# Attention with a token MLP: PSUM score banks as a group of three and a group of two plus one bank for VectorE, in place of two groups of three

## The chip, the cores and the metric

The kernel runs on one core of a Trainium2 chip. The metric is the time of one execution on the device in microseconds (us), the median of the runs. Five engines of the core work side by side, each through its own instruction queue: TensorE (PE, matrix products; PEld is its weight loads), VectorE (DVE), ScalarE (ACT), GpSimd (POOL) and SyncE (SP), which issues the transfers (DMA). Matrix products land in PSUM, which this kernel uses as eight banks of 128 rows by 512 fp32 numbers. All other data on the core lie in SBUF.

## The reference

The input x has 2048 rows (tokens) of 640 numbers in bf16. One layer norm feeds an attention block and an MLP that mixes tokens; the MLP's result gates the attention's:

```
xn  = layernorm(x)                                  # no scale, no shift
q,k,v = split(xn @ wqkv)                            # 32 heads of 20 numbers
s   = concat(softmax(q k^T / sqrt(20)) v) @ wo
h   = layernorm(xn)                                 # h^T: 640 x 2048
y   = (gelu(h^T @ w1 + b1) @ w2 + b2)^T             # 2048 -> 1536 -> 2048 over tokens
out = x + s * silu(y)
```

The largest part is the exponential of the scores: 32 heads x 2048 x 2048 numbers.

## The kernel before

**The unit of work.** The heads are taken in 8 sets of four (`NG`, `GH`), the queries in 4 parts of 512 (`NTB`): 32 passes. In a pass the keys are 16 chunks of 128. One unit is one head, one chunk, one part of the queries: a score tile of 128 keys by 512 queries, which fills one PSUM bank. There are 32 x 16 x 4 = 2048 units. A product of depth 32 (L1206, in `emit_st`) makes the tile; the four heads of a set lie in the four row groups of TensorE, so that tiles of different heads can be computed at once and tiles of the same head follow each other. Below, a "score phase" is one call of `emit_st`: the tiles that are issued together.

**Two ways to the exponential.** ScalarE takes the tiles of a whole bank group with one ACTIVATE (L1235, in `emit_exp`), which reads two or three adjacent banks and writes bf16 to `pt_sb`. VectorE takes single tiles and makes the exponential from bit patterns: one TENSOR_SCALAR from PSUM to 16-bit integers (L1246, `emit_op1`; one per unit), and after the four heads of a chunk three TENSOR_SCALARs over all four tiles at once (L1268, `emit_top`), which give three shifted copies. A chunk handled in this way is here called a VectorE chunk; it costs TensorE 16 value products in place of 4. Only the chunks in `RC` (five of a pass's 16) can be VectorE chunks. The value products (L1284, `emit_pv`) collect a pass in one bank.

**Banks.** Bank 6 (`AB`) collects the value products. Bank 7 (`JB`) serves all other products (MLP, projections, output), called jobs, one at a time. Banks 0 to 5 hold score tiles in two groups of three, `ACT_GROUPS`. A group is refilled (`do_st`, L1836) when ScalarE has read it. At the refill the planner may lend the group's last bank to VectorE: then two tiles go to ScalarE and the third to VectorE (`lent`). It lends if VectorE's reckoned backlog (`dve_load`, L1830) is below `LEND` and a VectorE chunk has a head left that the other two tiles don't use. A group with a lent bank can be refilled only when VectorE has read its tile (the test in `pe_cands`, L1665). Besides, VectorE may get a tile in bank 7 when no job holds it (`d_bank`, L1161), with the refill of a group or in a score phase of its own.

**Ramp and tail.** In the first part of the kernel (`ramp`) the layer norm, the transposes and the first projections run. Once the first score tile can be made, the group banks are withdrawn from the jobs. `dveready` is set when the keys of the first set are complete, and `ramp` ends when the last of the first value projections and the last of the first query projections are issued. While `ramp` holds there are neither lent banks nor tiles in bank 7, so VectorE gets no tile. At the end, banks 0 to 5 go to the last output products (`tbank`).

**Who sets the order.** The program is written out ahead of time by a planner (`schedule`). It keeps a clock for each engine with a reckoned cost for each instruction and picks the next instruction by priorities and readiness. On the chip the queues run in that fixed order with semaphores between them. Every 16 score tiles (`WIN`) the planner reads the next row of a table (`PLAN`, 129 rows, applied by `tune`, with the choices of `OPTS`), which sets its 14 options anew: among them `LEND` (the fifth digit of a row), `DRIDE` (how long TensorE may wait so that a tile for VectorE can ride with a refill), `CONFL` (whether a tile that rides may share its head with another of the phase), `PARTS` (value products taken in parts) and `DON` (whether new VectorE chunks may start). The weight loads of the MLP are reckoned at 1.8 times their bytes (`dma_w1`, `dma_w2`: 922 per row of 512 bytes).

Of the kernel before, what the change touches and what calls it, by code (L numbers as in the profile page):

```python
# [260 lines left out]
class _Kern:  # L261
# [4 lines left out]
    NG = 8  # L266
    EPS = 1e-5
    RP = 20
    ACT_GROUPS = ((0, 1, 2), (3, 4, 5))
    AB = 6  # L270
    JB = 7
    RC = (2, 5, 8, 11, 14)
# [12 lines left out]
    CONFL = True  # L285
    FILL, FGAP, FACT = True, 40.0, 0.6
    LATE = 2.0
    LEND, LEND_MIN = 1800.0, 3
    SHARE = True
    VPRIO = 24.0  # L290
    QAT = (0.0, 0.0, 0.0, 0.0)
# [10 lines left out]
        ("MINJ", (640.0, 320.0, 1000.0)),  # L302
        ("ROOM", (3, 6, 0)),
        ("DRIDE", (400.0, 150.0, 700.0)),
        ("LEND", (1800.0, 1300.0, 2400.0, 700.0, 0.0)),
        ("PARTS", ((2,), (2, 1), (3, 1), (1,), ())),
        ("LATE", (2.0, -9.0, 99.0)),
        ("DON", (True, False)),
# [5 lines left out]
        ("GROT", (1, 0)),  # L314
    )
    PLAN = (
        "00000000000010", "00000000000000", "00100000001000", "00000000000000", "10200300000100", "10200300100100",
        "20020000000010", "20022010000010", "10000000000100", "00000100000000", "01000100000100", "00000000000000",
        "20102000000000", "00000000000000", "00000000010000", "01000300010000", "01002310100110", "01010300110000",
        "01010320100000", "01021310100000", "01001310000100", "10000200010000", "10022210011000", "11022220011000",  # L320
        "00103300000010", "00102300000010", "21102000000000", "00000200000010", "20200000000000", "10201000000000",
        "10000200010000", "12000000010000", "00000000000000", "01000000000100", "01022300000100", "00022300010100",
        "02000010000010", "00000000000000", "00200010100010", "00000010110010", "01003000000100", "01000200010100",
        "01000200010100", "10000000100000", "10000010100100", "10100010000100", "01010020011100", "00000000000000",
        "01000200000000", "00000000000000", "00010000110000", "01010010110000", "21010310111000", "22110310111010",
        "00003100001000", "01000000000100", "01000000101100", "01010000101100", "00000000000000", "10000000010100",
        "01000000001110", "00000000001100", "00000000000000", "00001000000000", "22020000000000", "00000000000000",
        "01000000100000", "02000010100000", "01000010100000", "00000000000000", "01000300000000", "11020300000100",
        "11020300000000", "11120100000000", "11120100000010", "11120100010110", "11210100011110", "12210100011110",
        "02210100011010", "11210100001010", "11221100011010", "11201100111010", "11201210111110", "10020420000000",  # L330
        "00000000000000", "02000001010000", "30000000011000", "00000420000000", "00000400000100", "00100000100000",
        "01000200000000", "01000200000000", "00000000000000", "00023000101000", "01000000001000", "00100000000100",
        "00000000000000", "00000020000000", "00000000000000", "00001010000010", "01100000000000", "10000000000000",
        "00000000000000", "00000020100000", "10002320100000", "10200010001000", "10202010001000", "01200110011100",
        "00002000100000", "02002000010000", "00022020010000", "00000000000000", "00001001010100", "00001000111100",
        "00010420000000", "02001000001100", "00000000000000", "20000000100000", "00000300000000", "00104310000000",
        "00000100100010", "10020100100010", "30000100100010", "00002000001000", "01012000000000", "00000000000000",
        "00000320000000", "00022310000000", "00022311000000",
    )
    PARTS = (2,)  # L340
    DX = (1, 2, 3)
# [74 lines left out]
    def schedule(self):  # L416
# [14 lines left out]
        PROW = 4096  # L431
        A_x, A_wqkv, A_wo, B_w1, B_b1, B_w2, B_b2, out = (self.A_x, self.A_wqkv, self.A_wo, self.B_w1,
                                                          self.B_b1, self.B_w2, self.B_b2, self.out)
        AB, JB = self.AB, self.JB
        RC, NR = self.RC, len(self.RC)
        sl = {}

# [11 lines left out]
        done = set()  # L449
# [516 lines left out]

        jobs = []
        bankq = []
        freebanks = [3, 4, 5, 0, 1, 2, JB]
        retired = set()  # L970
        busybanks = set()
        active = []
# [85 lines left out]
        dquads = []  # L1058
        tfree = list(range(self.NTILE))
        dlive = [0]  # L1060
        dop1 = []
        lent = set()
        dtop = []
# [58 lines left out]
        def a_left(q):  # L1122
            n = sum(4 for c in range(NB) if (q, c) not in claimed)
            if a_cur[1] is not None and a_cur[0] == q:
                n += GH - a_cur[2]
            return n
# [34 lines left out]
        def d_bank():  # L1161
            if not dveready[0]:
                return None
            if JB in bank_off:
                return None
            if self.SHARE and JB in freebanks and len(dop1) < 2 and not ramp[0]:
                return JB
            return None

        def d_take(g, bk):  # L1170
            d = d_cur[0]
            if d is None:
                q, c, r = d_claimable()
                claimed.add((q, c))
                dlive[0] += 1
                d = d_cur[0] = dict(q=q, c=c, r=r, todo=[0, 1, 2, 3], tl=[tfree.pop(0), None, None, None], fin=[0.0] * 4, left=4, pk=0)
                stats["dve_units"] += 4
                nd_pass[q] += 1
            d["todo"].remove(g)
            if bk == JB:  # L1180
                freebanks.remove(bk)
                busybanks.add(bk)
            else:
                lent.add(bk)
            dop1.append((d, g, bk))
            u = (d["q"], d["c"], g)
            if not d["todo"]:
                d_cur[0] = None
            return u
# [52 lines left out]
        def emit_op1():  # L1242
            d, g, bk = dop1.pop(0)
            w = dt_sb[:, d["tl"][0], g, :]
            src = ps(bk)
            tk = pr.dve(lambda e: e.tensor_scalar(w, src, WOFF, 0.0, ALU.add, ALU.max), reads=[bank_slot[bk]],  # L1246
                   writes=[S_(f"dt{d['tl'][0]}_{g}")], name=f"dw{d['q']}_{d['c']}_{g}", cost=601.0)
            if bk != JB:
                lent.discard(bk)
            else:  # L1250
                busybanks.discard(bk)
                freebanks.append(bk)
                freebanks.sort(reverse=True)
            d["left"] -= 1
            if d["left"] == 0:
                dtop.append([d, 1])
                d["fin"][0] = tk.fin
                if self.EARLY:
                    dquads.append((0.0, d))
# [394 lines left out]
        def fin_bank(b):  # L1654
            return b not in busybanks
# [273 lines left out]
        while True:  # L1929
            guard += 1  # L1930
            if nclaim[0] >= win * self.WIN:
                self.tune(win)
                win += 1
            assert guard < 400000
            if ramp[0] and "v0_14" in done and "qk0_0_3" in done:
                ramp[0] = False
            if not dveready[0] and "qk0_1_3" in done:
                dveready[0] = True
            nomore = next_chunk(a_cur[0], claimed) is None and a_cur[1] is None
            if nomore:  # L1940
                for b in act_banks:
                    if b not in bank_off and b not in lent and not any(b in x[1] for x in pexp):
                        bank_off.add(b)
                        if len(tbank) < 4:
                            done.add(f"tbank{len(tbank)}")
                            tbank.append(b)
            if (nomore or (a_cur[0] == NP - 1 and a_left(NP - 1) < self.D_GUARD)) and d_cur[0] is None and not dop1:
                if not bankq and JB not in busybanks and JB not in bank_off:
                    bank_off.add(JB)
                    done.add(f"bankoff{JB}")  # L1950
            activate()
            order = sorted(("pe", "act", "dve", "pool"), key=lambda e: pr.T[e])
            cs_by = {}
            for e in order:
                cs_by[e] = pe_cands(pr.T[e]) if e == "pe" else eng_cands(e, pr.T[e])
            bt = None
            for e in order:
                if not cs_by[e]:
                    continue
                r = min(max(x[1], pr.T[e]) for x in cs_by[e])  # L1960
                if bt is None or r < bt[0]:
                    bt = (r, e)
            if bt is None:
                break
            r, e = bt
            ok = [x for x in cs_by[e] if x[1] <= r + 1e-6]
            ok.sort(key=lambda x: (x[0], x[1]))
            if pr.T[e] < r:
                pr.T[e] = r
            ok[0][2]()  # L1970
# [41 lines left out]
```

## Time and profile before

| | before |
|---|---|
| median of three runs | 756.44 us (755.57 to 756.48) |
| the profiled execution | 755.57 us, span 753.7 us |
| ScalarE busy | 729.9 us (97%) |
| VectorE busy | 721.0 us (96%) |
| TensorE busy | 717.6 us (95%) |
| exponentials of three banks on ScalarE | 208 |
| exponentials of two banks on ScalarE | 464 |
| score tiles of VectorE | 496 (124 chunks) |
| DMA, mean | 56 GB/s |

The span runs from the first to the last instruction; the time of the execution is 1.9 us longer. "Busy" counts overlapping instructions once. "Idle before" is time in which an engine had nothing to do ahead of an instruction, with what ended it. Matmuls of different row or column groups overlap, so that a busy TensorE is not one at its peak.

### The profile page before, as it was taken

The numbers are of one execution on the slowest core, as the hardware profiler recorded it, in microseconds if no ns is written. First come the engines' busy times: TensorE is split into PE (matmuls) and PEld (weight loads), VectorE is DVE, ScalarE is ACT, GpSimd is POOL, SyncE is SP. The second block draws the span as 40 slices with busy tenths as digits, with TensorE's granted clock in tenths as the row PEclk, the third lists the DMA queues.
The fourth block names the chain that finished last, engine by engine and source line by source line (L and its number), as shares of the span: only waits on it lengthen the run. The fifth ranks groups of instructions, "written<-read, shape, count | busy, mean of one in ns | idle before, by whom it ended". The sixth has DMA issues, their size and how long they took to land.

```text
span 753.7 us, 23158 instructions
## 1 busy us (share of the span) xinstructions
PE 717.6 (95%) x10302; PEld 240.7 (32%) x10302; DVE 721.0 (96%) x1320; ACT 729.9 (97%) x695; POOL 15.6 (2%) x22
## 2 busy tenths in 40 slices
PE   9999999999999999999999999999999988998997
PEld 7432223222323232323223323233333232222222
DVE  8869999999999999999999999999999999999997
ACT  4999999999999999999999999999999999999993
POOL 4200000000000000000000000000000000000001
PEclk9999999999999999999999999999999999999999
DMA  9584111110313031121014022223124340011011
GB/s 245 109 167 57 38 26 38 20 36 7 86 14 77 13 68 38 35 61 21 7 37 111 26 49 52 47 54 102 44 57 82 76 150 11 6 47 48 13 47 36
DMA packets 117143, 42.54 MB, mean 56 GB/s; under 512 B 75300, under 2 KB 115876, under 8 KB 116996
## 3 DMA queue, kind: packets, MB, share of 16 engines
q1 hardware_dynamic: 117044, 41.07, 23.9%
q8 instruction: 80, 1.31, 0.7%
q14 instruction: 19, 0.16, 0.1%
HBM read 26.37 MB, written 10.22 MB: 49 GB/s over the span
## 4 chain that ended last, share of the span: by engine, by line
ACT 85%; PE 12%; DVE 2%; DMA 1%; issue 0%; POOL 0%
ACT pt_sb L1235 83%; PE ps_all L1284 4%; PE ps_all L644 4%; PE ps_all L1206 4%; ACT zt_sb L840 1%; ACT zt_sb L835 1%; PE ps_all L929 1%; DMA xnT_sb<-regC 1%; DVE bst_sb L531 0%; DVE bst_sb L533 0%; DMA regA<-in_A_x_dram 0%; DVE regC L549 0%; DVE regC L1607 0%; PE ps_all L683 0%; DVE xnT_sb L611 0%
## 5 line engine op out<-in xcount | busy, mean ns | idle before, releaser
L1235 ACT ACTIVATE pt_sb<-ps_all 128x1024 bf16<-128x1024 f32 (+1 forms) x672 | 710.5, 1226 | 2.4 <-PE ps_all L1206 1.9
L1246 DVE TENSOR_SCALAR dt_sb<-ps_all 128x512 uint16<-128x512 f32 x496 | 328.2, 684 | 10.1 <-PE ps_all L1206 8.3
L1206 PE MATMUL ps_all<-qk_sb 32*128 32x512 bf16 x2048 | 266.7, 384 | 27.7 <-ACT pt_sb L1235 24.8
L1268 DVE TENSOR_SCALAR dt_sb<-dt_sb 128x2048 uint16<-128x2048 uint16 x372 | 241.9, 687 | 1.4
L1206 PEld LDWEIGHTS ps_all<-qk_sb 32*128 32x128 bf16 x2048 | 67.0, 91 | 283.8 <-ACT pt_sb L1235 231.8
L1284 PE MATMUL ps_all<-dt_sb,vs_sb 128*21 128x512 bf16 x1488 | 124.6, 382 | 0.8 <-DVE dt_sb L1268 0.7
L1284 PE MATMUL ps_all<-pt_sb,v_sb 128*21 128x512 bf16 x1552 | 124.2, 382 | 0.9 <-DVE tr_sb L1400 0.6
L644 PE MATMUL ps_all<-regB,regA 128*32 128x128 bf16 (+1 forms) x1536 | 68.2, 301 | 0.7 <-DVE regB L845 0.3
L644 PE MATMUL ps_all<-regC,regA 128*32 128x512 bf16 (+1 forms) x1536 | 68.4, 301 | 0.0
L1284 PE MATMUL ps_all<-dt_sb,v_sb 128*21 128x512 bf16 x496 | 49.0, 384 | 0.3 <-DVE tr_sb L1400 0.2
L644 PE MATMUL ps_all<-xnT_sb,wqk_sb 128*32 128x512 bf16 x640 | 48.2, 382 | 0.3 <-DVE zt_sb L814 0.2
L1284 PEld LDWEIGHTS ps_all<-dt_sb,vs_sb 128*21 128x21 bf16 x1488 | 31.5, 91 | 41.3 <-issue 21.9
L1284 PEld LDWEIGHTS ps_all<-pt_sb,v_sb 128*21 128x21 bf16 x1552 | 28.7, 90 | 47.7 <-issue 38.0
L644 PEld LDWEIGHTS ps_all<-regB,regA 128*32 128x32 bf16 x1536 | 27.2, 96 | 27.0 <-issue 13.1
L644 PEld LDWEIGHTS ps_all<-regC,regA 128*32 128x32 bf16 x1536 | 27.3, 96 | 25.6 <-issue 13.4
L929 PE MATMUL ps_all<-wv_sb,xnT_sb 128*128 128x128 bf16 (+3 forms) x160 | 29.5, 302 | 0.1
L644 PE MATMUL ps_all<-wv_sb,xnT_sb 128*32 128x480 bf16 x320 | 23.0, 369 | 0.0
L1400 DVE STREAM_TRANSPOSE tr_sb<-ps_all 128x512 f32<-128x512 f32 x31 | 22.1, 711 | 0.9 <-PE ps_all L1284 0.7
L644 PEld LDWEIGHTS ps_all<-xnT_sb,wqk_sb 128*32 128x32 bf16 x640 | 13.7, 95 | 18.2 <-issue 7.7
L1284 PEld LDWEIGHTS ps_all<-dt_sb,v_sb 128*21 128x21 bf16 x496 | 12.6, 90 | 21.3 <-issue 14.7
L814 DVE TENSOR_SCALAR zt_sb<-ps_all,b2h_sb 128x512 bf16<-128x512 f32 (+1 forms) x32 | 17.2, 544 | 0.0
L1044 DVE CAST v_sb<-ps_all 128x480 bf16<-128x480 f32 (+1 forms) x22 | 13.4, 610 | 3.3 <-PE ps_all L737 3.1
(82 smaller groups left out, 307.0 us busy)
## 6 DMA issues: line engine op xcount, KB each, us to landing
regA<-in_B_w_dram SPq DMA_DIRECT2D x6, 1024.0 KB
regA<-in_B_w_dram SPq DMA_DIRECT2D x8, 768.0 KB
qk_sb<-qk_scratch_dram SPq DMA_DIRECT2D x56, 80.0 KB
qk_scratch_dram<-qs_sb SPq DMA_DIRECT2D x32, 128.0 KB
regA<-in_A_x_dram SPq DMA_DIRECT2D x6, 640.0 KB
ok_scratch_dram<-on_sb SPq DMA_DIRECT2D x96, 20.0 KB
out_dram<-regC SPq DMA_DIRECT2D x3, 640.0 KB
wqk_sb<-in_A_wqkv_dram SPq DMA_DIRECT2D x2, 480.0 KB
```

The source lines that it names most:

```text
L644: fns.append(lambda e, c=c, e_=e_: e.matmul(oc(c, e_), lhsT[:, c:e_], rhs, start=start, stop=stop, tile_position=(0, c)))
L814: steps.append(("dve", lambda e, z=z, i=i, jj=jj: e.tensor_scalar(z[:, c0:c0 + n], ps(bk, n, i * n), 0.5, bias[:, jj:jj + 1], ALU.mult, AL ...
L835: steps.append(("act", lambda e: e.activation(tt_, tt_, AF.Tanh, scale=1.5957691216), [stt], [stt], f"th{j}", ac(n)))
L840: steps.append(("act", lambda e: e.activation(tt_, z, AF.Tanh), sz, [stt], f"th2_{j}", ac(n)))
L929: steps.append(("pe", lambda e, c=c, k=k: e.matmul(ap, oT_sb[0:k, c, b * 128:(b + 1) * 128], wo_ap[0:k, c, c0:c0 + n], start=(opens and c ...
L1044: return lambda e: e.tensor_copy(dst, src)
L1206: pr.pe(lambda e, outp=outp, lhsT=lhsT, rhs=rhs, g=g: e.matmul(outp, lhsT, rhs, start=True, stop=True, tile_position=(32 * g, 0)), reads=[ ...
L1235: tk = pr.act(lambda e: e.activation(outp, inp, AF.Exp, scale=math.log(2.0) / 128.0), reads=[bank_slot[b] for b in banks[:n]], writes=[S_( ...
L1246: tk = pr.dve(lambda e: e.tensor_scalar(w, src, WOFF, 0.0, ALU.add, ALU.max), reads=[bank_slot[bk]], writes=[S_(f"dt{d['tl'][0]}_{g}")], n ...
L1268: tk = pr.dve(lambda e: e.tensor_scalar(dst, src, dk, None, ALU.add), reads=[S_(f"dt{b0}_{g}") for g in range(4)], writes=[S_(f"dt{b}_{g}" ...
L1284: pr.pe(lambda e: e.matmul(outp, lhsT, rhs, start=(k == 0), stop=last, tile_position=(0, 32 * g)), reads=reads, writes=[bank_slot[AB]], na ...
L1400: steps.append(("dve", lambda e: e.transpose(tr_sb[:, :], ps(AB)), [bank_slot[AB]], [S_("tr")], f"epT{q}", 632.0))
```

## The change

Banks 0 to 5 are divided anew: ScalarE has a group of three (0, 1, 2) and a group of two (3, 4), and bank 5 becomes `DB`, a bank for VectorE's tiles alone. `d_bank` offers it first, whenever it is empty, without asking whether the ramp has ended. Until `dveready` is set, bank 5 serves jobs; after that it is withdrawn from them. The group of three may still lend its third bank (`LEND_MIN` is 3), the group of two never. At the end bank 5 joins the banks of the last output products.

The table is another one throughout: all 129 rows differ, and the choices for `LEND` are now 900, 300, 1500, 0 and 2500 ns in place of 1800, 1300, 2400, 700 and 0. Of the 129 rows before, 95 chose 1800, 18 chose 2400, 11 chose 1300, 4 chose 700 and 1 chose 0. After, 82 choose 900, 17 choose 1500, 16 choose 0 (never lend), 8 choose 2500 and 6 choose 300. Three rows before forbid new VectorE chunks (`DON`), none after. The reckoned weight loads are the same in both versions.

```diff
-    ACT_GROUPS = ((0, 1, 2), (3, 4, 5))
+    ACT_GROUPS = ((0, 1, 2), (3, 4))
+    DB = 5
...
-    LEND, LEND_MIN = 1800.0, 3
+    LEND, LEND_MIN = 1100.0, 3
...
-        ("LEND", (1800.0, 1300.0, 2400.0, 700.0, 0.0)),
+        ("LEND", (900.0, 300.0, 1500.0, 0.0, 2500.0)),
...
     PLAN = (
-        "00000000000010", "00000000000000", "00100000001000", "00000000000000", "10200300000100", "10200300100100",
+        "00010000000000", "00000000000000", "00000000000010", "00000000000000", "01020420000000", "01210300000000",
...
-        freebanks = [3, 4, 5, 0, 1, 2, JB]
+        freebanks = [3, 4, DB, 0, 1, 2, JB]
...
+        dbank = ["free"]
...
         def d_bank():
             if not dveready[0]:
                 return None
-            if JB in bank_off:
+            if DB in bank_off:
                 return None
+            if dbank[0] == "free" and fin_bank(DB):
+                return DB
             if self.SHARE and JB in freebanks and len(dop1) < 2 and not ramp[0]:
                 return JB
             return None
...
-            if bk == JB:
+            if bk == DB:
+                dbank[0] = "full"
+            elif bk == JB:
...
-            if bk != JB:
+            if bk == DB:
+                dbank[0] = "free"
+            elif bk != JB:
                 lent.discard(bk)
...
             if not dveready[0] and "qk0_1_3" in done:
                 dveready[0] = True
+                withdraw([DB])
...
+                if DB not in bank_off:
+                    bank_off.add(DB)
+                    done.add(f"tbank{len(tbank)}")
+                    tbank.append(DB)
```

## The prediction

> **What bounds the kernel now.** I read the page's busy shares first, then the groups of instructions with different shapes kept apart, then the busy time by stretches, and last the timeline of one refill.
>
> ```profile
> span 753.7 us, 23158 instructions
> PE 717.6 (95%) x10302; PEld 240.7 (32%) x10302; DVE 721.0 (96%) x1320; ACT 729.9 (97%) x695; POOL 15.6 (2%) x22
> L1235 ACT ACTIVATE pt_sb<-ps_all 128x1024 bf16<-128x1024 f32 x464 | 450.7, 1089 | 0.5 <-PE ps_all L1206 0.2
> L1246 DVE TENSOR_SCALAR dt_sb<-ps_all 128x512 uint16<-128x512 f32 x496 | 328.2, 684 | 10.1 <-PE ps_all L1206 8.3
> L1235 ACT ACTIVATE pt_sb<-ps_all 128x1536 bf16<-128x1536 f32 x208 | 301.2, 1530 | 1.9 <-PE ps_all L1206 1.7
> L1268 DVE TENSOR_SCALAR dt_sb<-dt_sb 128x2048 uint16<-128x2048 uint16 x372 | 241.9, 687 | 1.4
> ```
>
> Three engines are at 95% or more. ScalarE waited 2.4 us in all before its 672 exponentials: from the first to the last it never pauses, so the time is the work given to ScalarE, plus a ramp before and a tail behind. The units add up: 464 x 2 + 208 x 3 = 1552 on ScalarE, 496 on VectorE, 2048 together. The page gives the two forms of L1235 together as 710.5 us busy.
>
> ```profile
> core 0: us, PE busy (x) PEld busy (x) DVE busy (x) ACT busy (x) POOL busy (x), PEclk, DMA share, GB/s
> 15.60:38.00 22.40, 20.22 (x210) 9.80 (x208) 18.94 (x70) 22.35 (x18) 5.05 (x4) 1.00 0.63 113
> 38.00:49.80 11.80, 10.33 (x86) 3.84 (x87) 6.53 (x17) 10.98 (x9) 0.00 (x0) 1.00 0.80 206
> 60.00:738.00 678.00, 650.87 (x9654) 207.08 (x9646) 664.42 (x1159) 677.34 (x650) 0.63 (x1) 1.00 0.20 47
> ```
>
> In the long middle (60 to 738 us) ScalarE is idle for 0.7 us, VectorE for 678.00 - 664.42 = 13.6 us, TensorE for 27.1 us. Those two idle times are all the slack that there is. From 38.0 to 49.8 us VectorE is idle for 5.3 us; its first score tile begins at 49.82 us.
>
> ```profile
> 300.72 0.39 PE L1206 MATMUL ps_all<-qk_sb 32*128 32x512 bf16 x3
> 301.04 0.40 PE L1284 MATMUL ps_all<-dt_sb,v_sb 128*21 128x512 bf16 x4
> 301.19 0.69 DVE L1246 TENSOR_SCALAR dt_sb<-ps_all 128x512 uint16<-128x512 f32 x1 [0.17 <-PE ps_all L1206]
> ...
> 616.91 0.60 PE L1206 MATMUL ps_all<-qk_sb 32*128 32x512 bf16 x4 [0.41 <-ACT pt_sb L1235]
> 617.45 0.61 PE L1299 MATMUL ps_all<-wp_sb,zw_sb 128*21 128x512 bf16 x8
> ...
> 619.60 0.40 PE L1206 MATMUL ps_all<-qk_sb 32*128 32x512 bf16 x4
> 619.92 0.40 PE L1299 MATMUL ps_all<-wp_sb,zw_sb 128*21 128x512 bf16 x4
> ```
>
> A phase of three tiles takes TensorE 301.04 - 300.72 = 0.32 us. One of four takes the same where no head is doubled (619.60 to 619.92), and 0.54 us in the other case (616.91 to 617.45), so I price a doubled head at 0.22 us. A tile for VectorE is ready for it 0.47 us after its phase began (300.72 to 301.19), and VectorE reads it for 0.69 us: a bank of its own turns over in 1.16 us at best.
>
> **Prices.** The third bank adds 1530 - 1089 = 441 ns to an exponential. From 710.5 us = 672 f + 1552 x 0.441 us, the fixed part of an exponential is f = 0.039 us. A unit on ScalarE costs 710.5 / 1552 = 0.458 us on average, a chunk of four 1.83 us. An exponential of two banks takes 2 x 0.441 + 0.039 = 0.92 us of the queue, one of three 1.36 us. VectorE's chunk costs 4 x 328.2 / 496 + 3 x 241.9 / 372 = 4.60 us. If VectorE loses w us to waiting it gives up c chunks to ScalarE; the kernel gets 1.83 c longer, and VectorE has that time too: 4.60 c + 1.83 c = w. So one lost us of VectorE costs 1.83 / 6.43 = 0.28 us, provided that the table moves chunks and doesn't let ScalarE wait.
>
> **The number of exponentials.** Refills now alternate between three and two banks, 2.28 us for a pair. The own bank needs 1.16 us between refills. Behind an exponential of two banks the next refill comes after 0.92 us, too early, so I let it take one tile in each pair. With n pairs, a share s of the three-bank groups lent, and bank 7 giving 32 tiles as now (496 - 464): n + s n + 32 = 496, and 5 n - s n = 1552. Adding both gives n = 336, s n = 128: 672 exponentials, the number of today. Cost 0. Without any lending n = 310, 52 fewer exponentials, -2.0 us; with the own bank used in every second pair only, 5.5 n = 2016, n = 366.5 and 733 exponentials, +2.4 us.
>
> The Trainium skill, page "ScalarE: Activation LUTs", section "What ACT_TABLE_LOAD costs", gives an ACTIVATE with immediate operands 186 ns beside its elements, of which back-to-back ones overlap by 93 ns; that leaves 93 ns for each further exponential, against 39 ns from this trace's rows. As an estimate by this page, the term would be 0 as well, with -4.8 to +5.7 us around it; it speaks for few wide exponentials, which neither split has by itself.
>
> **The ramp.** The own bank is offered as soon as the first keys are complete, and lent banks and bank 7 only after the ramp. VectorE casts the last of those keys at 38.03 us, so the 5.3 idle us up to 49.8 can now be filled: -5.3 x 0.28 = -1.5 us. Bound on one side 0 (TensorE has 1.5 us idle there and jobs to run), on the other the whole idle time of VectorE from 15.6 on, 3.5 + 5.3 = 8.7 us, -2.5 us, since until then bank 5 also serves as a second job bank. The transposes by DMA that gate these jobs stay as they are.
>
> **VectorE's supply.** Before, its next tile could come with every refill, from either group: 30 waits, 8.3 us, 0.28 us each. After, the refill of the two-bank group can bring a tile only into bank 5, and that bank may not be empty. The backlog below which the third bank is lent falls from mostly 1800 to mostly 900 ns, that is from three to one and a half instructions of 0.6 to 0.7 us, while the next group of three comes 2.28 us later. So VectorE should run dry more often. No row shows how often. Lower bound 0; upper bound one more wait of 0.28 us for each of 124 chunks, 34.7 us, x 0.28 = +9.9 us. I take every second chunk, 17.4 us, +5.0 us, because the 2.28 us lie on the far side of the 900 ns but one tile per pair arrives in any case. That is more than VectorE's 13.6 us of slack, and that slack is already made of such waits.
>
> **TensorE.** A tile that rides with a full group of three makes four tiles, and one of the group's three heads is doubled unless the chunk's missing head is just the fourth. 336 - 128 = 208 groups are full. While fewer than 27.1 / 0.22 = 123 phases double a head, TensorE's idle time covers it. If that cover is gone, ScalarE waits, behind it nothing else. Lower bound 0; if all 208 double, 45.8 - 27.1 = 18.7 us. I take cover for most, and let ScalarE's 1.9 us of waits for L1206 double: +1.9 us.
>
> **What costs nothing.** MLP, projections, norms and output keep their instructions and their one job bank; their evictions lie within VectorE's busy time. No DMA is added on SyncE's queue, GpSimd gets none, and transfers run at a mean of 56 GB/s beside the middle stage. The tail has its four banks in both versions; 0.
>
> **The sum.** -1.5 + 0 + 5.0 + 1.9 = +5.4 us on the profiled execution's own 755.57 us, 761.0. That execution is the fastest of the runs, 0.87 us under their median, so against the median I predict 761.8 us.
>
> **Rivals.**
>
> First, the own bank feeds VectorE well: no lending (-2.0), the ramp filled (-1.5), no further waits. 756.44 - 3.5 = 752.9 us, faster. For it: a tile can wait in bank 5 without holding up a group, and 1.16 us of turnover is less than the 1.45 us or so that VectorE needs for a unit (721.0 / 496). Against it: refills come at fixed times, and 52 spared exponentials are worth little. It decides if VectorE's added waiting stays under 12 us, since 3.5 / 0.28 = 12.5.
>
> Second, TensorE becomes the bound: more than 123 doubled heads. At 160 it is 37 x 0.22 = 8.1 us over its slack, and ScalarE waits for that: 756.44 + 3.5 (ramp and supply) + 8.1 = 768.0 us. For it: TensorE's 95%. Against it: the planner may refuse such riders (25 of 129 rows do, by the tenth digit).
>
> Third, the split hardly matters: the table still lends often, 8 rows up to 2500 ns, so that bank 5 merely adds to it. Then 733 exponentials at +2.4, no added waits, the ramp -1.5: 757.3 us, no measurable change.
>
> **How the numbers follow.** Chances: the forecast 0.47, TensorE as the bound 0.17, hardly any difference 0.14, well fed 0.22. Hence faster by over 0.2% 0.22, within 0.2% 0.14, slower 0.64; 0.2% (1.5 us) is about what can be told from no change. The forecast's own range is 758 to 767: waits between a fifth of the chunks and all of them. The range of 8 in 10 goes from 752, near all gains at once (-2.5 - 2.0 = -4.5), to 772, the second rival at about 180 doubled heads; beyond either end I leave some 1 in 10.
>
> **What would show it.** Right: L1246's first start near 40 us; about 670 exponentials of L1235, near 210 of three banks; more than 8.3 us of waits of L1246 for L1206, some 25; fewer than 496 tiles on VectorE, 484 or so; ScalarE's idle time before L1235 at a few us. Wrong: as many tiles or more on VectorE and fewer exponentials (the first rival), or tens of us of ScalarE idle before L1235 with TensorE busy over 97% (the second). If the ramp moved later, or the tail, the whole sum misses its place.

## The result and the profile after

The changed kernel takes 760.96 us (median of four runs, 760.59 to 762.24), against 756.31 us for the kernel before in the same comparison: ratio 1.0066, 95% interval 1.0049 to 1.0084. It is slower, by about 4.7 us. The prediction was 761.8 us. One execution of 3378.1 us, in the run of the section on the lull in the ramp of the kernel before, lies outside all the others and is left out below.

The page's head for the changed kernel, as shown before for the old one:

```profile
span 759.2 us, 22924 instructions
PE 730.3 (96%) x10194; PEld 247.2 (33%) x10194; DVE 720.7 (95%) x1319; ACT 732.2 (96%) x683; POOL 15.7 (2%) x22
```

Its groups of instructions with shapes kept apart (line 1235 is now 1241, 1246 is 1252, 1206 is 1212, 1284 is 1292):

```profile
L1241 ACT ACTIVATE pt_sb<-ps_all 128x1024 bf16<-128x1024 f32 x425 | 429.7, 1078 | 4.6 <-PE ps_all L1212 3.6 <-PE ps_all L1292 0.3
L1241 ACT ACTIVATE pt_sb<-ps_all 128x1536 bf16<-128x1536 f32 x234 | 350.5, 1498 | 2.2 <-PE ps_all L1212 2.0
L1252 DVE TENSOR_SCALAR dt_sb<-ps_all 128x512 uint16<-128x512 f32 x496 | 332.8, 683 | 16.5 <-PE ps_all L1212 15.1
L1212 PE MATMUL ps_all<-qk_sb 32*128 32x512 bf16 x2048 | 290.0, 385 | 18.6 <-ACT pt_sb L1241 14.0 <-DVE dt_sb L1252 0.9
```

ScalarE and VectorE have the same shares of the units as before, to the tile: 425 x 2 + 234 x 3 = 1552 and 496. There are 13 fewer exponentials. VectorE's waits for score tiles went from 8.3 to 15.1 us, ScalarE's idle time before its exponentials from 2.4 to 6.8 us, and the score products now keep TensorE busy for 290.0 us in place of 266.7.

The busy time by stretches: length, busy time of PE, PEld, DVE, ACT and POOL with their instructions, then the granted clock of TensorE, the DMA share and GB/s. First the short stretches around two places, then the long ones of the prediction:

```profile
20.00:24.00 4.00, 4.00 (x30) 1.15 (x28) 1.94 (x11) 2.01 (x3) 1.01 (x1) 0.57 0.10 18
640.00:646.00 6.00, 5.05 (x58) 1.42 (x59) 6.00 (x12) 6.00 (x6) 0.00 (x0) 1.00 0.95 322
646.00:651.00 5.00, 3.71 (x45) 1.15 (x42) 3.50 (x6) 4.33 (x5) 0.00 (x0) 1.00 0.05 16
651.00:655.00 4.00, 3.61 (x16) 0.91 (x15) 3.52 (x8) 3.02 (x4) 0.00 (x0) 0.62 0.00 2
```

```profile
38.00:49.80 11.80, 11.74 (x111) 4.54 (x111) 11.72 (x30) 11.06 (x13) 0.00 (x0) 1.00 0.84 130
60.00:738.00 678.00, 658.27 (x9522) 213.93 (x9519) 656.63 (x1144) 673.76 (x627) 0.63 (x1) 1.00 0.20 46
```

From 38.0 to 49.8 us VectorE, once idle for 5.3 us, is idle for 0.1. But from 20 to 24 us TensorE has 0.57 of its clock, and ScalarE is busy for only 2.01 of the 4 us. The same follows at 651 to 655 us, at a clock of 0.62; before, the clock was 1.00 in the stretches shown. What lies behind the second place is seen in the chain of work that ended last (start, length and what):

```profile
641.29 4.87 DMA oT_scratch_dram<-stage_sb
646.18 3.04 DMA xnT_sb<-oT_scratch_dram
```

SyncE's timeline of the same stretch (start, length, what):

```profile
635.91 2.46 SPq L1560 DMA_DIRECT2D regA<-in_A_x_dram  x4
641.29 0.34 SPq L1432 DMA_DIRECT2D oT_scratch_dram<-stage_sb  x1
646.18 0.67 SPq L892 DMA_DIRECT2D xnT_sb<-oT_scratch_dram  x1
```

And TensorE's, where the second line is held by that reload:

```profile
647.58 0.39 PE L1212 MATMUL ps_all<-qk_sb 32*128 32x512 bf16 x3
649.26 0.39 PE L930 MATMUL ps_all<-wv_sb,xnT_sb 128*128 128x512 bf16 x1 [1.29 <-DMA xnT_sb<-oT_scratch_dram]
```

SyncE issues four reloads of x (640 KB each, for the residual) from 635.91 us on. A store of attention output at 641.29 us stands behind them and takes 4.87 us; the reload that needs it starts only at 646.18, and TensorE, which works off its queue in the written order, stands for 1.29 us at an output product, until 649.26 us. ScalarE runs dry, and the clock falls afterwards. Before, the reloads of x were issued at 607.5 us, since the MLP's last products, which they wait for, came earlier, and the reload of attention output followed the same store after 2.1 us (SyncE's timeline of the kernel before):

```profile
607.50 2.98 SPq L1552 DMA_DIRECT2D regA<-in_A_x_dram  x4
...
638.03 0.36 SPq L1424 DMA_DIRECT2D oT_scratch_dram<-stage_sb  x1
640.17 0.67 SPq L891 DMA_DIRECT2D xnT_sb<-oT_scratch_dram  x1
```

At the first place TensorE waits for the transposed rows of the layer norm (its timeline):

```profile
18.29 0.39 PE L1212 MATMUL ps_all<-qk_sb 32*128 32x512 bf16 x3 [0.41 <-ACT pt_sb L1241]
19.79 0.72 PE L630 MATMUL ps_all<-xnT_sb,wp_sb 128*128 128x256 bf16 x5 [1.11 <-DMA xnT_sb<-regC]
```

and ScalarE, in its own timeline, for TensorE:

```profile
22.49 3.28 ACT L1241 ACTIVATE pt_sb<-ps_all 128x1024 bf16<-128x1024 f32 x3 [1.99 <-PE ps_all L1212]
```

So the total came out as forecast, but the trace points at two short places that the forecast doesn't name. I put this as theory A: the loss is made there. Theory B is the forecast's own: it is spread over the middle, from VectorE's supply and from doubled heads.

### The profile page after: what moved, and what is told of

Same layout as the page of the kernel before. It is cut to its first block, busy times and chain, and to the rows that moved or that the text cites. A ratio compares the mean times of both kernels' runs of the same rounds, so it can differ in the third digit from the quotient of the medians.

```text
span 759.2 us, 22924 instructions
## 1 busy us (share of the span) xinstructions
PE 730.3 (96%) x10194; PEld 247.2 (33%) x10194; DVE 720.7 (95%) x1319; ACT 732.2 (96%) x683; POOL 15.7 (2%) x22
## 4 chain that ended last, share of the span: by engine, by line
ACT 74%; PE 20%; DVE 3%; DMA 2%; POOL 0%; issue 0%
ACT pt_sb L1241 72%; PE ps_all L1212 6%; PE ps_all L1292 5%; PE ps_all L645 5%; PE ps_all L930 1%; PE ps_all L1317 1%; ACT zt_sb L841 1%; PE ps_all L630 1%; DVE dt_sb L1252 1%; DMA xnT_sb<-regC 1%; DMA oT_scratch_dram<-stage_sb 1%; ACT zt_sb L836 1%; DVE dt_sb L1276 1%; DMA xnT_sb<-oT_scratch_dram 0%; POOL st_sb L567 0%; DVE regC L1615 0%
## 5 line engine op out<-in xcount | busy, mean ns | idle before, releaser
L1241 ACT ACTIVATE pt_sb<-ps_all 128x1024 bf16<-128x1024 f32 (+1 forms) x659 | 712.3, 1227 | 6.8 <-PE ps_all L1212 5.6
L1252 DVE TENSOR_SCALAR dt_sb<-ps_all 128x512 uint16<-128x512 f32 x496 | 332.8, 683 | 16.5 <-PE ps_all L1212 15.1
L1212 PE MATMUL ps_all<-qk_sb 32*128 32x512 bf16 x2048 | 290.0, 385 | 18.6 <-ACT pt_sb L1241 14.0
L1276 DVE TENSOR_SCALAR dt_sb<-dt_sb 128x2048 uint16<-128x2048 uint16 x372 | 246.5, 687 | 1.7
L1212 PEld LDWEIGHTS ps_all<-qk_sb 32*128 32x128 bf16 x2048 | 74.6, 91 | 279.1 <-ACT pt_sb L1241 187.1
L645 PE MATMUL ps_all<-regC,regA 128*32 128x512 bf16 (+1 forms) x1536 | 66.1, 301 | 0.0
L645 PEld LDWEIGHTS ps_all<-regB,regA 128*32 128x32 bf16 x1536 | 28.9, 96 | 25.6 <-issue 11.3
L930 PE MATMUL ps_all<-wv_sb,xnT_sb 128*128 128x128 bf16 (+3 forms) x160 | 31.3, 310 | 1.3 <-DMA xnT_sb<-oT_scratch_dram 1.3
L1292 PEld LDWEIGHTS ps_all<-dt_sb,v_sb 128*21 128x21 bf16 x496 | 12.6, 90 | 23.8 <-issue 17.4
```

The source lines that it names most:

```text
L645: fns.append(lambda e, c=c, e_=e_: e.matmul(oc(c, e_), lhsT[:, c:e_], rhs, start=start, stop=stop, tile_position=(0, c)))
L930: steps.append(("pe", lambda e, c=c, k=k: e.matmul(ap, oT_sb[0:k, c, b * 128:(b + 1) * 128], wo_ap[0:k, c, c0:c0 + n], start=(opens and c ...
L1212: pr.pe(lambda e, outp=outp, lhsT=lhsT, rhs=rhs, g=g: e.matmul(outp, lhsT, rhs, start=True, stop=True, tile_position=(32 * g, 0)), reads=[ ...
L1241: tk = pr.act(lambda e: e.activation(outp, inp, AF.Exp, scale=math.log(2.0) / 128.0), reads=[bank_slot[b] for b in banks[:n]], writes=[S_( ...
L1276: tk = pr.dve(lambda e: e.tensor_scalar(dst, src, dk, None, ALU.add), reads=[S_(f"dt{b0}_{g}") for g in range(4)], writes=[S_(f"dt{b}_{g}" ...
L1292: pr.pe(lambda e: e.matmul(outp, lhsT, rhs, start=(k == 0), stop=last, tile_position=(0, 32 * g)), reads=reads, writes=[bank_slot[AB]], na ...
```

## The experiments

### Closing the lull in the ramp

Products of zero weights go into TensorE's written-out queue, ahead of the product that waits at 18.7 us. No other instruction changes place.

```diff
+        i = next(n for n, t in enumerate(pe) if any(x.name == "xTd5" for x in t.waits.values()))
+        j = max(n for n in range(i) if pe[n].name == "pvz")
+        pe[i:i] = [_Task("pe", "pe", pe[j - 3 + n % 4].fn, "pvz") for n in range(16)]
```

> The changed kernel, with 16 more products of zero weights put into TensorE's queue just before the product that waits for the transposed rows at 18.7 us; nothing else is moved. Theory A (the loss is made at two places where TensorE waits for a transfer and its granted clock then falls): the clock from 20 to 24 us stays at 1.00 in place of 0.53 to 0.62, ScalarE's 2.0 us of idle time at 20.5 us goes, and the time falls by 1.5 to 2.0 us, to about 759.2. Theory B (the forecast's: the loss is spread over the middle, from VectorE's supply and TensorE's doubled heads): 761.0, within 0.5 us of the changed kernel.

Measured: 760.09 us, ratio to before 1.0056 (1.0042 to 1.0070). The clock from 20 to 24 us was 1.00, and ScalarE was busy for 3.07 us there in place of 2.01. The gain over the changed kernel is 0.9 us, under what theory A expected, and the intervals overlap; measured from the runs of the kernel before in each comparison it is only 0.2 us (4.65 to 4.42). In the profiled execution the collision at 640 us was worse, which may be where some of it went: the reload started 5.94 us after the store (639.06 to 645.00), and TensorE waited for 2.6 us behind it.

### Moving the reloads of x

```diff
+        x2 = [t for t in sp if t.name in ("x2_1", "x2_2", "x2_3")]
+        for t in x2:
+            sp.remove(t)
+        i = next(n for n, t in enumerate(sp) if t.name == "oTl70_4_48") + 1
+        sp[i:i] = x2
```

> The changed kernel, with three of the four reloads of x (640 KB each) put behind the reload of attention output in SyncE's queue; no other queue is touched. Theory A: the store at 641 us no longer stands behind 2.6 MB, the reload is issued about 2 us after it in place of 4.9, TensorE's 1.3 us of waiting at 648 us goes, the clock from 650 to 660 us is 1.00 in place of 0.83, ScalarE's 1.65 us of idle time from 650 to 655 goes, and the time falls by 2.0 to 3.5 us, to 757.5 to 759. Theory B: no change beyond 0.5 us.

Measured: 758.28 us, ratio 1.0029 (1.0018 to 1.0040), 2.7 us less than the changed kernel. SyncE's timeline:

```profile
634.53 0.42 SPq L1569 DMA_DIRECT2D regA<-in_A_x_dram  x1
639.91 0.34 SPq L1441 DMA_DIRECT2D oT_scratch_dram<-stage_sb  x1
641.76 0.68 SPq L901 DMA_DIRECT2D xnT_sb<-oT_scratch_dram  x1
642.49 2.16 SPq L1569 DMA_DIRECT2D regA<-in_A_x_dram  x3
```

and the stretches around it:

```profile
640.00:650.00 10.00, 8.31 (x82) 2.81 (x85) 9.47 (x17) 10.00 (x10) 0.00 (x0) 1.00 0.65 216
650.00:660.00 10.00, 9.65 (x89) 3.02 (x89) 10.00 (x20) 10.00 (x11) 0.00 (x0) 1.00 0.02 6
```

The reload starts 1.85 us after the store, the clock holds, and ScalarE is busy throughout. The runs spread from 756.79 to 760.0 us, and their mean clocks from 0.999 to 0.996. In the profiled one (757.44 us) the clock did not fall in the ramp either, although nothing was changed there (TensorE's timeline, then the stretch behind it):

```profile
19.31 0.72 PE L639 MATMUL ps_all<-xnT_sb,wp_sb 128*128 128x256 bf16 x5 [0.38 <-DMA xnT_sb<-regC]
20.00:24.00 4.00, 3.91 (x36) 1.41 (x37) 2.99 (x15) 3.59 (x4) 1.01 (x1) 1.00 0.16 31
```

So the fall in the ramp differs from one execution to the next, and the clock of 1.00 in the first experiment's single trace doesn't by itself show that the zero products held it. That the slower executions here lost their time in the ramp is inferred from their mean clocks; they have no trace.

### Both edits

> Both edits together, the 16 zero products in the ramp and the three reloads of x moved back. Theory A: 756 to 757.5 us, within 0.2% of the kernel before. Theory B: still near 761.

Measured: 756.62 us, ratio 1.0016 (1.0007 to 1.0025). Of the 4.7 us, 1.0 us is left; two edits that touch neither the bank split nor the table took the rest. Theory B is out as the main cause. The stretches of this kernel:

```profile
20.00:24.00 4.00, 3.91 (x36) 1.53 (x35) 2.42 (x13) 3.07 (x4) 1.01 (x1) 1.00 0.09 17
651.00:655.00 4.00, 3.71 (x34) 1.19 (x27) 4.00 (x9) 4.00 (x5) 0.00 (x0) 1.00 0.02 4
60.00:738.00 678.00, 658.10 (x9543) 214.54 (x9547) 659.36 (x1149) 676.07 (x630) 0.63 (x1) 1.00 0.20 47
```

Against the second kernel the ramp's filling is worth 758.28 - 756.62 = 1.7 us by the medians and 1.1 us by the means (758.09 and 757.00), with intervals that overlap, and it isn't a full cure: three of the 11 executions still took 758.0 to 758.2 us at mean clocks of 0.996 to 0.998. Against the first, the moved reloads are worth 760.09 - 756.62 = 3.5 us by the medians (3.0 by the means), and every execution here (758.23 us at most) is faster than any of the first experiment (759.31 at least).

### The same collision in the kernel before

Two reloads of x are held back until the data of the store at 638 us is ready, and issued ahead of it.

```diff
+        x2 = [t for t in sp if t.name in ("x2_2", "x2_3")]
+        for t in x2:
+            sp.remove(t)
+        i = next(n for n, t in enumerate(sp) if t.name == "oTst26")
+        x2[0].waits["dve"] = sp[i].waits["dve"]
+        sp[i:i] = x2
```

> The kernel before, with two of its four reloads of x (1.3 MB) held back until the data of the store at 638 us is ready, and issued ahead of that store; no other queue is touched. Theory A: the store lands some 3 us later, TensorE waits for the reload behind it, ScalarE runs dry for 1 to 2 us and the granted clock falls: 2 to 4 us longer, 758.5 to 760.5. Theory B: a wait of this size stays within TensorE's and ScalarE's cover, under 1 us longer.

Measured: 761.46 us, ratio 1.0073 (1.0061 to 1.0086): 5.8 us longer, more than the 2 to 4 expected, and as slow as the changed kernel, from one place in SyncE's queue. The reload started 5.88 us after the store (639.57 to 645.45), more than the 4.9 us of the changed kernel, and TensorE waited for 4.3 us. SyncE's timeline, and after it the stretches:

```profile
639.57 0.45 SPq L1434 DMA_DIRECT2D oT_scratch_dram<-stage_sb  x1
645.45 0.66 SPq L901 DMA_DIRECT2D xnT_sb<-oT_scratch_dram  x1
```

```profile
640.00:650.00 10.00, 5.52 (x63) 1.41 (x64) 6.12 (x10) 5.88 (x6) 0.00 (x0) 0.88 0.43 151
650.00:660.00 10.00, 9.77 (x85) 2.64 (x81) 8.46 (x16) 8.79 (x9) 0.00 (x0) 0.78 0.00 0
```

ScalarE lost 4.1 us in the first of these stretches and 1.2 us in the second, which sums to the 5.8 us of the comparison but for 0.5. That the 1.3 MB held the store up longer than the 2.6 MB did, with its issue only 1 us behind them, fits a store that gets its turn behind them; but SyncE also waited for 3.4 us until the reloads of x had landed, before it came to the reload of attention output. I did not separate the two.

### The wait or the clock

The kernel of the first experiment, with 32 more zero products in front of the output product that waits at 648 us. The transfers stay.

```diff
+        i = next(n for n, t in enumerate(pe) if any(x.name == "oTl70_4_48" for x in t.waits.values()))
+        j = max(n for n in range(len(pe)) if pe[n].name == "pvz")
+        pe[i:i] = [_Task("pe", "pe", pe[j - 3 + n % 4].fn, "pvz") for n in range(32)]
```

> The changed kernel with the 16 zero products in the ramp (as in the first of these runs, 760.1 us) and 32 more just before the product that waits for the reload at about 648 us; the reloads of x stay where they are, so the wait itself stays. If the fall of the clock is the larger part of that loss: the clock from 640 to 660 us is 1.00, ScalarE's idle time there falls from 2.5 us to under 1.5, and the time to about 758.5. If the wait itself is the larger part: within 0.5 us of 760.1.

Measured: 758.37 us, ratio 1.0032 (1.0022 to 1.0042). TensorE is kept busy through most of the wait (32 products, 645.47 to 647.38), ScalarE still runs dry once for 1.45 us, but the clock stays at 1.00 afterwards. From 760.09 to 758.37 is 1.7 us for the clock; from there to 756.62 is another 1.75 us for the wait itself. The run comes from another comparison than the other two, though: measured from each comparison's own kernel before (4.42, 2.29 and 0.95 us over it) the shares are 2.1 and 1.3 us, and by ScalarE's idle time from 640 to 660 us (2.5, 1.45 and 0 us in the three profiled executions) 1.0 and 1.45. Both parts are there, each about half of the loss; which is the larger is not settled.

### A lull in the ramp of the kernel before

The last 23 warming products, which the kernel issues up to 18.5 us and nobody reads, are left out.

```diff
+        w = [t for t in pe[:i] if t.name == "warm"][-23:]
+        self.prog.tasks["pe"] = [t for t in pe if t not in w]
```

> The kernel before without the last 23 of the warming products that it issues up to 18.5 us, whose results nothing reads. If a lull of TensorE of about 1 us at 18 us is what makes the clock fall in the changed kernel: the clock from 18 to 24 us falls to 0.5 to 0.8 here too, and the time rises by 1 to 2 us, to about 757.2. If the fall belongs to the two-bank group or to the bank of VectorE's own: the clock stays 1.00 and the time within 0.3 us of the kernel before.

Measured: 756.2 us, ratio 1.0002 (0.9992 to 1.0011): a miss on the whole. In the profiled execution TensorE stood for 1.35 and 0.88 us, and the clock stayed at 1.00 (TensorE's timeline, then the stretch behind it):

```profile
17.52 0.39 PE L1214 MATMUL ps_all<-qk_sb 32*128 32x512 bf16 x3 [1.35 <-ACT pt_sb L1243]
18.79 0.28 PE L637 MATMUL ps_all<-xnT_sb,wp_sb 128*128 128x256 bf16 x1 [0.88 <-DMA xnT_sb<-regC]
```

```profile
20.00:24.00 4.00, 3.37 (x37) 1.48 (x35) 3.05 (x9) 4.00 (x5) 0.79 (x1) 1.00 0.25 50
```

Two of the nine executions compared took 757.46 and 757.56 us at a mean clock of 0.995, the others 755.53 to 756.25 us at 0.997 to 1.000. But the unchanged kernel, run beside it, did the same in two of 17 (757.4 and 757.79 us, 0.995). So a pause of about 1 us at this place isn't enough by itself to bring the fall about, and a lower mean clock comes without it too (where in the kernel, no trace of those executions shows). What stands for the zero products is the third experiment against the second, 1.1 to 1.7 us; why the changed kernel's ramp loses its clock stays open. One thing differs between its two traces without zero products: TensorE's wait for the transposed rows was 1.11 us where the clock fell and 0.38 us where it held. The first pause of this experiment, 1.35 us, is longer than either and the clock held, so this isn't the whole condition. The Trainium skill, page "TensorE: Matmul & The Clock Gate", section "What's actually happening", says that the gate looks at a free-running window of about 3.4 us. That agrees with a fall that comes in some executions of one program only, but the fall here came without an idle stretch of that length (the longest wait ahead of it was 1.11 us in the ramp, 1.29 us at 649 us); no run here shows the window itself.

### The split without the table

To see what the two splits are worth by themselves, the table is emptied in both, and every option keeps its first value: lending below 1800 ns before, below 900 ns after.

```diff
-    PLAN = ( ... )
+    PLAN = ()
```

In the split after, the default for lending goes with it:

```diff
-    LEND, LEND_MIN = 1100.0, 3
+    LEND, LEND_MIN = 900.0, 3
```

> The split before (two groups of three), without the table: every option keeps its first value throughout, lending below 1800 ns. Forecast's theory (the split itself decides): this is faster than the new split without a table, by some 5 us. Rival (the split by itself is worth nothing, both need their own lending threshold): the two within 2 us of each other. Either way about 10 us over the kernel before.

> The split after (three, two and a bank for VectorE), without the table: every option keeps its first value throughout, lending below 900 ns. Forecast's theory: some 5 us slower than the split before without a table, with more waits of VectorE for score tiles. Rival: within 2 us of it. The ramp of this one can lose about 2 us by the clock, as the changed kernel's does.

Measured: 763.42 us (ratio 1.0097, 1.0082 to 1.0112) for the split before, 765.68 us (1.0124, 1.0107 to 1.0141) for the split after. Both give VectorE 488 tiles. Their groups of VectorE's first instruction, the split before and then the split after:

```profile
L1223 DVE TENSOR_SCALAR dt_sb<-ps_all 128x512 uint16<-128x512 f32 x488 | 321.4, 679 | 21.9 <-PE ps_all L1183 19.8
```

```profile
L1229 DVE TENSOR_SCALAR dt_sb<-ps_all 128x512 uint16<-128x512 f32 x488 | 325.2, 680 | 29.3 <-PE ps_all L1189 28.0
```

The new split makes VectorE wait for 8.2 us more, the sign that the forecast gave its supply term. The times differ by 2.3 us, nearer to the rival's "within 2 us" than to 5 us. The intervals of the ratios overlap, but the executions don't (762.95 to 764.27 and 765.34 to 766.22 us), so the new split, with its threshold, is a little slower here. In these two traces neither loss of the changed kernel appears: the clock is 1.00 from 20 to 24 and from 640 to 660 us, and with the new split the reloads of x (651.31 us) come behind the store (647.61) and its reload (649.49). The collision belongs to the written-out order, not to the split as such. What the bank split does to the time by itself is therefore small.

### The lending threshold of each split

```diff
-    LEND, LEND_MIN = 1100.0, 3
+    LEND, LEND_MIN = 1800.0, 3
```

That is the split after; in the split before the same line goes from 1800 to 900. The table is empty in both.

> The split after, without the table, lending below 1800 ns in place of 900. The forecast's step on VectorE's supply says that the lower threshold lets VectorE run dry: with 1800 its waits for score tiles fall from 28.0 us, it takes more than 488 tiles, and the time falls below 765.7 us, to about 762. Rival: with a bank of its own, 900 is already enough, and a higher threshold gives VectorE more than it can work off, so that ScalarE's group of three waits for the lent bank: VectorE's waits fall, but the time rises by over 10 us.

> The split before, without the table, lending below 900 ns in place of 1800. Both theories: without a bank of its own VectorE lives on lent banks, so it runs dry more often (over 30 us of waits for score tiles, against 19.8), takes fewer than 470 tiles, and the time rises by 5 to 15 us over 763.4. If the threshold hardly matters for this split either, it stays within 2 us.

Measured: the split after with 1800 ns takes 806.07 us (1.0660, 1.0629 to 1.0691). VectorE waits for only 14.2 us and takes 516 tiles, as both theories said, but the time rises by 40 us. The page's busy line of this kernel, and two late stretches:

```profile
PE 744.2 (92%) x10318; PEld 247.3 (31%) x10318; DVE 742.8 (92%) x1354; ACT 726.7 (90%) x700; POOL 15.6 (2%) x22
```

```profile
745.00:760.00 15.00, 10.18 (x312) 5.58 (x300) 6.05 (x16) 3.97 (x5) 0.00 (x0) 1.00 0.01 2
760.00:775.00 15.00, 13.18 (x68) 5.29 (x68) 9.60 (x19) 1.26 (x1) 2.26 (x2) 1.00 0.54 176
```

ScalarE doesn't stand waiting for lent banks, as I had written for the rival: 9.2 us of waits for score products in all. Its last exponential ends at 747.7 us, and then 57 us follow in which the MLP and the output products are made up. I take it that the extra chunks pushed these jobs behind the exponentials (VectorE's time, and 12 more value products each on TensorE); no run separates this. The rival's direction was right, its place wrong.

The split before with 900 ns takes 782.14 us (1.0344, 1.0314 to 1.0374), 444 tiles on VectorE and 58.4 us of waits, more than the 5 to 15 us that I had allowed. So of the two thresholds tried each split wants its own: without a bank for VectorE 1800 ns, with one, 900 ns does the same (488 tiles in both).

### Split and table one by one

> The new split with the table, the lending choices and the default of the kernel before. If the split carries the change of time, about 761 us as in the changed kernel. If the table is fitted to one split, well above both kernels, 780 us or more, with ScalarE waiting for tens of us.

> The split before with the table, the lending choices and the default of the changed kernel. If the table carries the change of time, about 761 us. If the table is fitted to one split, well above both kernels, 780 us or more, with VectorE taking far fewer than 496 tiles, since the table's lending thresholds are half as high.

Measured in one execution each: 817.06 us for the new split with the old table, 801.35 us for the old split with the new table. In the first, 508 tiles went to VectorE and the rest of the jobs ran on behind the exponentials again; in the second, VectorE got 412 tiles and waited 60.0 us for them, and ScalarE had the other 1636 units. Each table, with its lending choices, is fitted to one split, and no part of the 4.7 us can be put down to one of them alone. Much of the damage can be the threshold: without any table, the other split's threshold alone took the new split from 765.68 to 806.07 us and the old one from 763.42 to 782.14. (Of the two tables' 129 rows 125 differ in their digits, not all.)

## Why the prediction was right, and where it was right for the wrong reason

**Direction, size and range** held: +5.4 us forecast, +4.7 measured. The terms did not all hold, and that the total came out is in good part luck: about 3.7 of the 4.7 us were made at two places that the forecast doesn't name, while the +6.9 us that it put on VectorE's supply and on TensorE were hardly there.

**The number of exponentials** (0, between -2.0 and +2.4): 659 in place of 672, at 0.039 us each -0.5 us. The rate argument with one tile per pair of refills was good enough for the count. The saving itself doesn't show: all exponentials together kept ScalarE busy for 712.3 us, and for 711.4 with both places mended, against 710.5 before.

**The ramp** (-1.5): the mechanism is there in part. VectorE's first score tile begins at 40.71 us in place of 49.82, and its idle time from 38.0 to 49.8 us is 0.1 us. But VectorE took no tile more for it (496 both times): it gained 5.2 us here, and its waits for score tiles grew by 6.8 us. And the forecast missed that TensorE runs dry in the rearranged ramp at 18 us and that the clock can fall behind it: 1.1 to 1.7 us.

**VectorE's supply** (+5.0, half the chunks with one more wait) was mis-sized. Its waits rose by 6.8 us, not 17.4; at the forecast's 0.28 per us that is +1.9 us, or +1.4 with both places mended (13.2 - 8.3 = 4.9 us, the group of VectorE's waits of that kernel). Nor did VectorE give up chunks: 496 tiles, not 484, so the price of 0.28, which is paid in chunks that go to ScalarE, wasn't paid. The reason given was right only in direction: without a table the new split has 28.0 us of these waits at 900 ns and 14.2 at 1800 ns. But fewer waits were not less time: 1800 ns gave VectorE so much that the kernel took 40 us longer.

**TensorE** (+1.9): the score products cost 290.0 - 266.7 = 23.3 us more, and the cover held. TensorE's idle time from 60 to 738 us fell only from 27.1 to 19.7 us, and with both places mended ScalarE waited for score products for 2.0 us, against 1.9 before. This term was nearly 0, and the second rival, TensorE as the bound, did not come about.

**What costs nothing** is the step that failed. The forecast said that no DMA is added on SyncE's queue and that the transfers are light beside the middle stage, and left it there. None was added, but the MLP's last products came later, so the reloads of x were issued at 635.9 us in place of 607.5 and fell on a store and a reload that TensorE's queue waits for. Mending that place is worth 2.7 to 3.5 us. A mean of 56 GB/s says nothing about 2.6 MB in one stretch: DMA engines were busy to 0.95 from 640 to 646 us.

**The sum after the fact.** The first four experiments were compared with runs of the kernel before at 755.67 us, 0.6 us under those of the result, so a term taken across the two is no better than that. From there +1.0 us stays with both places mended, 1.7 us comes from the ramp's clock (758.28 - 756.62; 1.1 by the means) and 2.7 us from the second place (760.96 - 758.28). What is left of the forecast's terms (+1.4 for VectorE's waits, -1.5 for the ramp, -0.5 for the exponentials) sums to -0.6, so it doesn't give the +1.0. What does can be read on ScalarE, from the start of its first exponential to the end of its last, in the profiled executions of the kernel before (span 753.7 us) and of the kernel with both edits (754.9 us); the fourth busy time is ScalarE's:

```profile
15.62:742.21 726.59, 695.56 (x10125) 225.68 (x10123) 702.43 (x1264) 724.62 (x687) 5.69 (x5) 1.00 0.23 52
13.90:744.74 730.84, 708.30 (x10064) 234.75 (x10079) 702.38 (x1268) 726.84 (x677) 6.38 (x6) 1.00 0.23 52
```

The first exponential starts 1.7 us earlier, and the tail behind the last is 1.3 us shorter (10.2 us in place of 11.5), where the forecast had put 0. Between them ScalarE is busy for 2.2 us more and idle for 2.0 us more (4.0 in place of 2.0). The work is casts of the first projections that it now does in this stretch (2.1 us in place of 0.4) and 0.9 us more of exponentials. Together that is the 1.2 us between the two spans; the forecast had none of these terms. How low TensorE's activity must be for the clock to fall is not settled either, and the kernel before isn't quite free of falls.

## What to carry to other kernels

A schedule written out ahead of time can hold its mean loads and still lose at one point where a bulk transfer is issued just ahead of a small one that an in-order queue waits for; after a change of order, look at every issue of bulk data and ask which store or reload now stands behind it. A lull of TensorE can cost more than its length, when its clock falls after it, so a few products of zeros in front of a known wait can be cheaper than the wait alone. Options that a search has fitted to one layout of buffers can be worse than none on another (817 against 766 us and 801 against 763 us here): compare layouts with their own options, or with none.

## What was not expected of the hardware

The same ramp ran with and without a fall of the granted clock (0.57 from 20 to 24 us in the changed kernel's trace, 1.00 with the reloads moved), so a single profile may show or miss it. At the other place, about half of a loss of 3.5 us goes with a clock that fell when the wait was over (0.84 from 651 to 655 us in the first experiment's trace, 0.62 in the changed kernel's). And 32 products whose results add zeros, put into a wait, took away that half.
